# A spectral GFNet branch beside a gated ReGLU branch on one core: half-row passes grouped by three units, one ring of six PSUM banks, and 24 small copies issued by ScalarE

## The chip, the cores and the metric

The kernel runs on one core of one Trainium2 chip. The metric is the device time of one execution in microseconds (us). Three runs of the kernel before took 446.72, 446.89 and 446.91 us, a median of 446.89 us.

## What is computed

The reference adds three things: the input, a spectral filter of its layer norm, and a gated feed-forward block of its layer norm.

```python
def _A_ref(x, w_r, w_i):
    X = jnp.fft.rfft2(x, axes=(-2, -1)) * (w_r + 1j * w_i)
    return jnp.fft.irfft2(X, s=(S, D), axes=(-2, -1))

def _B_ref(x, W_gate, W_up, W_down):
    gate = jnp.einsum("bsd,df->bsf", x, W_gate)
    up = jnp.einsum("bsd,df->bsf", x, W_up)
    h = gate * (gate > 0) * up
    return jnp.einsum("bsf,fd->bsd", h, W_down)

xn = _layernorm(x, axis=-1)
return x + _A_ref(xn, A_w_r, A_w_i) + _B_ref(xn, B_W_gate, B_W_up, B_W_down)
```

S = 2048 rows, D = 448 columns, F = 1792 hidden columns, all in float32.

## The kernel before

**Arithmetic.** Every float32 operand of a matmul is split into a float16 high part and a float16 low part, and a product is three matmuls: high by high, high by low, low by high. A matmul streams up to 512 columns into one PSUM bank, which holds 512 float32 values in each of 128 partitions; there are 8 banks.

**The gated branch.** The rows are cut into four chunks of 512 (order 0, 2, 1, 3), the hidden columns into 14 tiles of 128, taken in groups of 5, 5 and 4. A *unit* is one hidden tile on one chunk: 56 units. A unit has two outputs, the gate (g = 0) and the up projection (g = 1), one bank each. D = 448 is three and a half contraction tiles, so an output takes 10 matmuls with all 128 rows (`SEQ`, line 706, issued by `gu_full`, line 712) and one with 64 rows, the *half pass* (`gu_half`, line 718). The half pass of the gate uses rows 0 to 63 of the array and that of the up projection rows 64 to 127 (`TOP`, line 707).

Units are taken in pairs (`mates`, line 969). The first of a pair, the *opener*, runs its 20 full matmuls; then four half passes stand together, two of its mate and two of its own (`gu_halves`, line 740); then the mate runs its 20 (`gu_unit`, line 730). I call the half passes that stand together a *stand*. There are 28 stands of four.

After a unit, `gu_post` (line 766) works on its outputs: ScalarE reads the gate bank and writes relu(gate) (line 752, "relu" below), VectorE reads the up bank and multiplies (line 756, "times"), ScalarE makes the high part (line 760) and VectorE the low part (line 764). When all units of a group and chunk are done, four down projections (`dn_mm`, line 775, lines 783 and 790) of 15 or 12 matmuls each use them.

**PSUM.** Units take a tile of two banks from a pool of two (`gu`), down projections one bank from a pool of two (`dn`, line 778), everything of the spectral branch one bank from a pool of two (`fx`, line 145): 4 + 2 + 2 banks.

**The spectral branch** is a list of background items (`bg`, from line 801): layer norm of chunks 1 and 3, transposes by DMA into the tiles `T`, discrete Fourier transforms as matmuls (lines 357 and 389), then butterflies on VectorE in four stages over 18 buffers (`bfly`, line 391), multiplication by the filter, the inverse butterflies, and the inverse transforms (lines 611 and 632). The butterfly with factor 1 (p = 0, lines 393 to 398) writes the sum into a free buffer and the difference over `b`, the second operand, and puts `a` at the end of the list of free buffers, from which the next one is popped. Two kinds of small copies inside the chip's memory are issued by SyncE: 16 row copies (`row_in`, line 559; the row that all blocks share) and, per pair of spectra, two exchange copies that mirror rows (`swap`, lines 544 and 545 before the filter, 547 and 548 behind it; line 548 is already ScalarE's).

**The order** is made at build time. Each matmul, VectorE and ScalarE step is issued by the program in the order of the units; background items are dealt out between them by a credit in us of VectorE time (`room`, line 1100, and the search for the share `load` in lines 1105 to 1110, which asks that the rooms of all units add up to the need of the background list), and a scheduler with its own cost model then sets the final order of each engine's queue. The opening (line 30) is an order written out by hand; it ends with the first units of chunk 0 and the stand named `hp4`. At run time each engine works through its own queue in that order and waits on semaphores.

Of the kernel before, what the change touches and what calls it, by code (L numbers as in the profile page):

```python
# [21 lines left out]
XW = 4 * GW  # L22
# [111 lines left out]
def tile_gfnet_reglu(ctx: ExitStack, tc: tile.TileContext, x, xr, wgu, wd, wf, wrow, ident, c_fd, c_fm, c_im, c_row, c_id,  # L134
# [10 lines left out]
    def fx():  # L145
        return psum.tile([128, 512], F32, name="fx", bufs=2)
# [184 lines left out]
    def ln_tp(n2, tiles):  # L331
        if n2 not in tp:
            tp[n2] = fx().bitcast(F16).rearrange("p (a b) -> p a b", b=128)
        for a in tiles:
            P.transpose(tp[n2][:, a, :], tt[n2][:, a, :], id_t)
# [9 lines left out]

    zps, eo, X, Xh, yps, cur = {}, {}, {}, {}, {}, {}

    def f_dft(n2):
        q, j = n2 % 4, n2 // 4
        js = slice(128 * j, 128 * (j + 1))  # L350
        ps = fx()
# [33 lines left out]
    def f_sdft(n2):  # L385
        y = yps[n2] = fx()[:, 0:XW].rearrange("p (g c k) -> p g c k", g=4, c=2)
# [4 lines left out]
    def bfly(a, b, p, sgn):  # L391

        if p == 0:
            t = free.pop()
            V.tensor_tensor(t, a, b, op=OP.add)  # L395
            V.tensor_tensor(b, a, b, op=OP.subtract)  # L396
            free.append(a)
            return t, b
        t = free.pop()
        if p == 4:  # L400
# [5 lines left out]
            free.append(b)  # L406
# [132 lines left out]
    def swap(key, k):  # L539
# [3 lines left out]
        if key == "X":  # L543
            nc.sync.dma_start(t[1:64], u[65:128])
            nc.sync.dma_start(t[64:128], u[0:64])
# [10 lines left out]
    def row_in(j):  # L556
        for par in range(2):
            p = 16 * j + 8 * par
            nc.sync.dma_start(row[p:p + 8, 0, :], cur["s1", j, par][64:65].rearrange("p g c k -> p (g c) k"))
# [7 lines left out]
    def row_dft(d):  # L567
        y = state["rowps"] = fx()
# [35 lines left out]
    def i_sdft(n2):  # L604
        ps = fx()
# [20 lines left out]
    def i_ddft(n2):  # L626
        ps = fx()
# [81 lines left out]
    def gu_open(f, q):  # L709
        hps[f, q] = psum.tile([128, 2, 512], F32, name="gu", bufs=2)  # L710

    def gu_full(f, q, gs, cs, start, stop, seq=SEQ):
        for g in gs:
            for i, (a, b) in enumerate(seq):
                last["P"] = P.matmul(hps[f, q][:, g, cs], wt[f, g][:, a, :], Tq[q][:, b, cs],  # L715
                                     start=(start and i == 0), stop=(stop and i == len(seq) - 1)).ins

    def gu_half(f, q, g, start, prev):
# [3 lines left out]
        m = P.matmul(hps[f, q][:, g, 0:512], wt[f, g][rows, 7, :], Tq[q][rows, b, :], start=start, stop=not start).ins  # L722
# [7 lines left out]
    def gu_unit(f, q, mate):  # L730
# [7 lines left out]
        gu_halves(f, q, mate)  # L738

    def gu_halves(f, q, mate):  # L740
        gu_open(*mate)
        m = last["P"]
        for i in range(4):
            with tc.high_priority(offset=2000 if i else 0):
                m = gu_half(*((f, q) if i > 1 else mate), 1 - i % 2, i < 2, m)
        opened.add(mate)
# [3 lines left out]
    def gu_relu(f, q):  # L750
        g1s[f, q] = mt([128, 512], F32, "g1", 3)
        last["A"] = A.activation(g1s[f, q], hps[f, q][:, 0, :], AF.Relu, scale=2.0 ** -22).ins  # L752

    def gu_times(f, q):
        g1 = g1s[f, q]
        last["V"] = V.scalar_tensor_tensor(g1, hps[f, q][:, 1, :], 2.0 ** -22, g1, op0=OP.mult, op1=OP.mult).ins  # L756
# [18 lines left out]
    def dn_mm(fs, n2, c0=0, c1=D):  # L775
        q, j = n2 % 4, n2 // 4
        js = slice(128 * j, 128 * (j + 1))
        ps = psum.tile([128, 512], F32, name="dn", bufs=2)
# [180 lines left out]
    gseq = [("gu", g, f, q) for g, fs in enumerate(groups) for q in CHUNKS for f in fs]  # L959
    units, pend = [], []  # L960
# [239 lines left out]
```

## Time and profile before

| | us |
|---|---|
| median of three runs | 446.89 |
| the profiled execution, its own time | 446.92 |
| its span, first to last instruction | 445.1 |
| TensorE busy | 438.4 (98%) |
| VectorE busy | 373.5 (84%) |
| ScalarE busy | 178.9 (40%) |
| GpSimd busy | 32.9 (7%) |

The 1.8 us between the span and the profiled time lie around the program. "Busy" of TensorE counts a matmul from its start to its modelled end, and successive matmuls overlap, so its pace is read from starts: how far the start of one group is from the start of the next. A weight load (PEld) is an instruction of its own that overlaps the matmul before it. Line numbers with an L are those of the kernel; a queue's own work (issuing a DMA) carries a q behind the engine.

### The profile page before, as it was taken

The page shows a single profiled execution, that of the slowest core. Times are in us where ns is not written, and L with a number is a line of the kernel's source. Part 1 is how long each engine was busy: PE and PEld are TensorE (multiplying, and loading weights), DVE is VectorE, ACT ScalarE, POOL GpSimd, SP SyncE. Part 2 cuts the span into 40 slices and gives each one's busy share as a digit, 9 for nine tenths or more (in the row PEclk, how much of TensorE's full clock was granted, in tenths as well). Part 3 has the DMA queues.
Part 4 walks back from the last instruction along what each step waited for, and adds up shares of the span by engine and source line. Part 5 has one row for each costly group of instructions (what it writes and reads, how often), then busy time and mean ns, then how long its engine had stood idle before and what let it go on. Part 6 is the DMA issues. An engine that isn't in the chain of part 4 may idle for free.

```text
span 445.1 us, 7091 instructions
## 1 busy us (share of the span) xinstructions
PE 438.4 (98%) x2630; PEld 218.8 (49%) x2630; DVE 373.5 (84%) x802; ACT 178.9 (40%) x365; POOL 32.9 (7%) x97
## 2 busy tenths in 40 slices
PE   8999999999999999999999999999999999999997
PEld 3543554444546444444444444444444455556565
DVE  5988696998858979999999999896997997766364
ACT  5886252351543666043233145344142242233230
POOL 2431031040000120000000010000000000000000
DMA  8929966041001261432220021000001333231113
GB/s 271 323 52 282 371 217 119 1 90 41 0 14 61 95 222 34 133 105 62 85 80 6 1 84 55 0 13 0 14 0 42 93 96 90 55 96 34 63 43 124
DMA packets 37115, 39.72 MB, mean 89 GB/s; under 512 B 17927, under 2 KB 32473, under 8 KB 37081
## 3 DMA queue, kind: packets, MB, share of 16 engines
q1 hardware_dynamic: 35928, 37.40, 27.4%
q10 hardware_dynamic: 1152, 1.87, 2.1%
q8 instruction: 20, 0.33, 0.3%
q14 instruction: 15, 0.11, 0.1%
HBM read 24.45 MB, written 3.67 MB: 63 GB/s over the span
## 4 chain that ended last, share of the span: by engine, by line
PE 91%; DVE 3%; DMA 2%; ACT 1%; issue 1%; POOL 1%; SPq 0%; ACTq 0%
PE gu L715 50%; PE dn L783 29%; PE gu L722 3%; PE fx L611 2%; PE fx L357 2%; PE fx L632 2%; PE fx L389 2%; DMA y<-in_xr 1%; DMA T<-tt 1%; DVE bst L248 1%; DVE wt L669 1%; DVE y L291 0%; DVE g L756 0%; ACT T L341 0%; DVE tt L320 0%
## 5 line engine op out<-in xcount | busy, mean ns | idle before, releaser
L715 PE MATMUL gu<-T,wt 128*128 128x512 f16 (+1 forms) x1140 | 256.1, 375 | 0.0
L715 PEld LDWEIGHTS <-wt 128*128 128x128 f16 x1140 | 108.7, 98 | 129.8 <-issue 9.3
L783 PE MATMUL dn<-wdt,h 128*128 128x448 f16 (+2 forms) x684 | 136.4, 349 | 0.0
L783 PEld LDWEIGHTS <-h 128*128 128x128 f16 x684 | 65.8, 98 | 59.9
L752 ACT ACTIVATE g<-gu 128x512 f32<-128x512 f32 x56 | 33.2, 594 | 115.1 <-PE gu L722 77.4
L760 ACT ACTIVATE h<-g 128x512 f16<-128x512 f32 x56 | 35.0, 627 | 47.3 <-DVE g L756 47.3
L756 DVE SCALAR_TENSOR_TENSOR g<-gu,g 128x512 f32<-128x512 f32 x56 | 38.5, 687 | 11.4 <-ACT g L752 11.3
L790 DVE SCALAR_TENSOR_TENSOR xy<-dn,dsc,xy 128x448 f32<-128x448 f32 (+2 forms) x49 | 32.9, 671 | 15.1 <-PE dn L783 14.8
L764 DVE TENSOR_TENSOR h<-g,h 128x512 f16<-128x512 f32 x56 | 38.5, 689 | 4.9 <-ACT h L760 4.8
L665 ACT ACTIVATE wt<-wst,wsc 128x512 f16<-128x512 f32 x28 | 19.1, 716 | 15.7 <-DVE wsc L196 15.7
L669 DVE SCALAR_TENSOR_TENSOR wt<-wst,wsc,wt 128x512 f16<-128x512 f32 x28 | 20.5, 749 | 0.0
L637 DVE SCALAR_TENSOR_TENSOR xy<-fx,fsc,xy 128x448 f32<-128x448 f32 x16 | 10.8, 681 | 10.7 <-PE fx L632 10.7
L189 POOL PARTITION_ALL_REDUCE wm<-wm x15 | 7.8, 521 | 158.9 <-ACT junk L186 158.9
L396 DVE TENSOR_TENSOR y<-y 128x456 f32<-128x456 f32 x22 | 13.9, 631 | 4.8 <-DMA row<-y 4.5
L722 PE MATMUL gu<-T,wt 64*128 64x512 f16 x112 | 17.0, 381 | 0.8 <-DMA T<-tt 0.7
L186 ACT ACTIVATE junk<-wst 128x512 bf16<-128x512 f32 x28 | 17.4, 622 | 0.2
L595 ACT ACTIVATE vt<-y,fsc 128x912 f16<-128x912 f32 x8 | 8.4, 1052 | 20.7 <-PE fx L611 12.3
L618 ACT ACTIVATE wf<-fx 114x512 f16<-114x512 f32 x16 | 9.4, 588 | 17.4 <-PE fx L611 16.6
L553 DVE TENSOR_TENSOR y<-y,sw 128x456 f32<-128x456 f32 x16 | 10.1, 628 | 5.7 <-DMA sw<-y 5.7
L395 DVE TENSOR_TENSOR y<-y 128x456 f32<-128x456 f32 x22 | 13.8, 628 | 0.2
L611 PEld LDWEIGHTS <-vt 128*128 128x128 f16 x192 | 12.0, 98 | 3.3
L611 PE MATMUL fx<-wf,vt 128*128 128x128 f16 x192 | 13.2, 219 | 0.0
(115 smaller groups left out, 431.4 us busy)
## 6 DMA issues: line engine op xcount, KB each, us to landing
wst<-in_wgu SPq DMA_DIRECT2D x28, 256.0 KB
wf<-in_wf SPq DMA_DIRECT2D x8, 456.0 KB
sw<-y SPq DMA_DIRECT2D x16, 224.4 KB
y<-in_xr SPq DMA_DIRECT2D x16, 224.0 KB
xy<-in_x SPq DMA_DIRECT2D x16, 224.0 KB
out<-xy SPq DMA_DIRECT2D x15, 224.0 KB
wdst<-in_wd SPq DMA_DIRECT2D x14, 224.0 KB
sw<-y SPq DMA_DIRECT2D x8, 228.0 KB
```

Of the source, the lines that this page charges most:

```text
L186: A.activation(o, src, AF.Square, scale=SQ, accum_out=acc)
L611: P.matmul(o, v[:, h, w], m[:, c, :], start=(i == 0), stop=(i == 2), skip_group_check=True)
L665: A.activation(w[:, 0:4, :], wst[f, g], AF.Copy, scale=wsc[f, g])
L669: V.scalar_tensor_tensor(w[:, 4:8, :], st, sc, w[:, 0:4, :], op0=OP.mult, op1=OP.subtract)
L715: last["P"] = P.matmul(hps[f, q][:, g, cs], wt[f, g][:, a, :], Tq[q][:, b, cs], start=(start and i == 0), stop=(stop and i == len(seq) - 1 ...
L722: m = P.matmul(hps[f, q][:, g, 0:512], wt[f, g][rows, 7, :], Tq[q][rows, b, :], start=start, stop=not start).ins
L752: last["A"] = A.activation(g1s[f, q], hps[f, q][:, 0, :], AF.Relu, scale=2.0 ** -22).ins
L756: last["V"] = V.scalar_tensor_tensor(g1, hps[f, q][:, 1, :], 2.0 ** -22, g1, op0=OP.mult, op1=OP.mult).ins
L760: A.activation(ht[f, q][:, 0, :], g1s[f, q], AF.Copy)
L764: V.tensor_tensor(h[:, 1, :], g1s.pop((f, q)), h[:, 0, :], op=OP.subtract)
L783: last["P"] = P.matmul(ps[:, 0:c1 - c0], ht[f, q][:, a, js], wdt[f][:, b, c0:c1], start=(i == 0), stop=(i == n - 1)).ins
L790: last["V"] = V.scalar_tensor_tensor(o, dps[n2][:, 0:c1 - c0], dsc[:, g:g + 1], o, op0=OP.mult, op1=OP.add).ins
```

## The change

Five edits.

1. `mates` now lists units in groups: two groups of two, sixteen of three, two of two (20 groups for 56 units). The opener's stand holds the half passes of both mates and its own: six in a stand of a group of three. Every later full matmul of a unit is ordered behind the last half pass issued. The down projections of a finished chunk are issued behind a mate instead of behind every second unit.
2. `gu` and `dn` share one ring of six banks (`RINGS`, `bank`); a unit takes two tiles of one bank.
3. The butterfly with factor 1 writes the difference over `a`, and the freed buffers go to the front of the list, so that they are reused last.
4. The 16 row copies and one of the two exchange copies before the filter (8) are issued by ScalarE.
5. The search for the share asks for 3.0 us more than the need.

```diff
--- before.py
+++ after.py
@@ -144,4 +144,7 @@

-    def fx():
-        return psum.tile([128, 512], F32, name="fx", bufs=2)
+    RINGS = {'gu': ('gu', 6), 'dn': ('gu', 6), 'fx': ('fx', 2)}
+
+    def bank(name="fx"):
+        tag, n = RINGS[name]
+        return psum.tile([128, 512], F32, name=name, tag=tag, bufs=n)

@@ -332,3 +335,3 @@
         if n2 not in tp:
-            tp[n2] = fx().bitcast(F16).rearrange("p (a b) -> p a b", b=128)
+            tp[n2] = bank().bitcast(F16).rearrange("p (a b) -> p a b", b=128)
         for a in tiles:
@@ -344,3 +347,2 @@

-
     zps, eo, X, Xh, yps, cur = {}, {}, {}, {}, {}, {}
@@ -350,3 +352,3 @@
         js = slice(128 * j, 128 * (j + 1))
-        ps = fx()
+        ps = bank()
         T = Tq[q]
@@ -385,3 +387,3 @@
     def f_sdft(n2):
-        y = yps[n2] = fx()[:, 0:XW].rearrange("p (g c k) -> p g c k", g=4, c=2)
+        y = yps[n2] = bank()[:, 0:XW].rearrange("p (g c k) -> p g c k", g=4, c=2)
         m, xh = fm_t[n2 % 8][:, n2 // 8], Xh[n2 % 8][:, n2 // 8]
@@ -395,5 +397,5 @@
             V.tensor_tensor(t, a, b, op=OP.add)
-            V.tensor_tensor(b, a, b, op=OP.subtract)
-            free.append(a)
-            return t, b
+            V.tensor_tensor(a, a, b, op=OP.subtract)
+            free.insert(0, b)
+            return t, a
         t = free.pop()
@@ -405,3 +407,3 @@
             V.tensor_tensor(a[:, :, 1], a[:, :, 1], b[:, :, 0], op=o1)
-            free.append(b)
+            free.insert(0, b)
             return t, a
@@ -544,3 +546,3 @@
             nc.sync.dma_start(t[1:64], u[65:128])
-            nc.sync.dma_start(t[64:128], u[0:64])
+            nc.scalar.dma_start(t[64:128], u[0:64])
         else:
@@ -558,3 +560,3 @@
             p = 16 * j + 8 * par
-            nc.sync.dma_start(row[p:p + 8, 0, :], cur["s1", j, par][64:65].rearrange("p g c k -> p (g c) k"))
+            nc.scalar.dma_start(row[p:p + 8, 0, :], cur["s1", j, par][64:65].rearrange("p g c k -> p (g c) k"))

@@ -567,3 +569,3 @@
     def row_dft(d):
-        y = state["rowps"] = fx()
+        y = state["rowps"] = bank()
         for d in ((0, 1), (2,))[d]:
@@ -604,3 +606,3 @@
     def i_sdft(n2):
-        ps = fx()
+        ps = bank()
         v, m = vt[n2 % 8][:, n2 // 8], im_t[n2 % 8][:, n2 // 8]
@@ -626,3 +628,3 @@
     def i_ddft(n2):
-        ps = fx()
+        ps = bank()
         h = pgh[n2]
@@ -709,3 +711,3 @@
     def gu_open(f, q):
-        hps[f, q] = psum.tile([128, 2, 512], F32, name="gu", bufs=2)
+        hps[f, q] = [bank("gu") for g in range(2)]

@@ -714,4 +716,6 @@
             for i, (a, b) in enumerate(seq):
-                last["P"] = P.matmul(hps[f, q][:, g, cs], wt[f, g][:, a, :], Tq[q][:, b, cs],
+                m = last["P"] = P.matmul(hps[f, q][g][:, cs], wt[f, g][:, a, :], Tq[q][:, b, cs],
                                      start=(start and i == 0), stop=(stop and i == len(seq) - 1)).ins
+                if "opened" in state and "half" in last:
+                    tc.add_manual_dep(m, last["half"].name, NOSYNC, reason="half passes stand together")

@@ -721,3 +725,3 @@
         rows, b = TOP[g]
-        m = P.matmul(hps[f, q][:, g, 0:512], wt[f, g][rows, 7, :], Tq[q][rows, b, :], start=start, stop=not start).ins
+        m = P.matmul(hps[f, q][g], wt[f, g][rows, 7, :], Tq[q][rows, b, :], start=start, stop=not start).ins
         if "opened" in state:
@@ -729,3 +733,3 @@

-    def gu_unit(f, q, mate):
+    def gu_unit(f, q, mates):

@@ -737,11 +741,15 @@
         gu_full(f, q, gs, cs, True, False)
-        gu_halves(f, q, mate)
+        gu_halves(f, q, mates)

-    def gu_halves(f, q, mate):
-        gu_open(*mate)
+    def gu_halves(f, q, mates):
         m = last["P"]
-        for i in range(4):
+        vs = [v[2:] for v in mates] + [(f, q)]
+        for i in range(2 * len(vs)):
+            v = vs[i // 2]
+            if i % 2 == 0 and v != (f, q):
+                gu_open(*v)
+                opened.add(v)
             with tc.high_priority(offset=2000 if i else 0):
-                m = gu_half(*((f, q) if i > 1 else mate), 1 - i % 2, i < 2, m)
-        opened.add(mate)
+                m = gu_half(*v, 1 - i % 2, v != (f, q), m)
+        last["half"] = m

@@ -751,3 +759,3 @@
         g1s[f, q] = mt([128, 512], F32, "g1", 3)
-        last["A"] = A.activation(g1s[f, q], hps[f, q][:, 0, :], AF.Relu, scale=2.0 ** -22).ins
+        last["A"] = A.activation(g1s[f, q], hps[f, q][0], AF.Relu, scale=2.0 ** -22).ins

@@ -755,3 +763,3 @@
         g1 = g1s[f, q]
-        last["V"] = V.scalar_tensor_tensor(g1, hps[f, q][:, 1, :], 2.0 ** -22, g1, op0=OP.mult, op1=OP.mult).ins
+        last["V"] = V.scalar_tensor_tensor(g1, hps[f, q][1], 2.0 ** -22, g1, op0=OP.mult, op1=OP.mult).ins

@@ -777,3 +785,3 @@
         js = slice(128 * j, 128 * (j + 1))
-        ps = psum.tile([128, 512], F32, name="dn", bufs=2)
+        ps = bank("dn")
         n = 3 * len(fs)
@@ -959,6 +967,11 @@
     gseq = [("gu", g, f, q) for g, fs in enumerate(groups) for q in CHUNKS for f in fs]
+    mates, inner, k = {}, set(), 0
+    for n in [2, 2] + [3] * 16 + [2, 2]:
+        mates[gseq[k]] = gseq[k + 1:k + n]
+        inner.update(gseq[k + 1:k + n])
+        k += n
     units, pend = [], []
-    for k, u in enumerate(gseq):
+    for u in gseq:
         units.append(u)
-        if k % 2 and pend:
+        if u in inner and pend:
             units += pend
@@ -968,3 +981,2 @@
     units += pend
-    mates = {u: v for u, v in zip(gseq[::2], gseq[1::2])}
     first = {}
@@ -1050,5 +1062,6 @@
     def gu_slab(f, g):
-        if f % 2 == 0 and g == 0:
+        first = ("gu", 0, f, q) in mates
+        if first and g == 0:
             gu_open(f, q)
-        gu_full(f, q, (g,), slice(0, 512), f % 2 == 0, f % 2 == 1)
+        gu_full(f, q, (g,), slice(0, 512), first, not first)

@@ -1064,4 +1077,4 @@
             piece(f"{tag}{f}", fn, f, q)
-        if f % 2 == 0:
-            piece(f"hp{f}", gu_halves, f, q, mates["gu", 0, f, q][2:])
+        if ("gu", 0, f, q) in mates:
+            piece(f"hp{f}", gu_halves, f, q, mates["gu", 0, f, q])
         for g in range(2):
@@ -1083,3 +1096,3 @@
         G.memset(warm, 0.0)
-        wps = psum.tile([128, 512], F32, name="dn", bufs=2)
+        wps = bank("dn")
         gu_open(0, q)
@@ -1108,3 +1121,3 @@
         need = sum(c - m * p for c, p, _, _ in bg)
-        lo, hi = (m, hi) if sum(room(i, m) for i in range(RAMP, last_gu)) < need else (lo, m)
+        lo, hi = (m, hi) if sum(room(i, m) for i in range(RAMP, last_gu)) < need + 3.0 else (lo, m)
     load[0] = hi
@@ -1124,3 +1137,3 @@
             run_bg(until=marks["T", q])
-            gu_unit(f, q, (mates.get(u) or (0, 0, None, None))[2:])
+            gu_unit(f, q, mates.get(u))
         else:
```

The program that results has as many instructions of each kind on each compute engine as before; the order differs. Lines are shifted: 722 becomes 726, 715 becomes 717, 783 becomes 791, 752 becomes 760, 632 becomes 634, 357 becomes 359.

**A stand of half passes, on TensorE.** `gu` are the banks of units (the number names the unit's tile), `wt` their weights, `T` the input chunk. Before, in the middle of the kernel's last third:

```order
L715 MATMUL gu_3639<-T2_63,wt_3174 128x512
L722 LDWEIGHTS wt_3222
L722 MATMUL gu_3660<-T2_63,wt_3222 128x512
L722 LDWEIGHTS wt_3219
L722 MATMUL gu_3660<-T2_63,wt_3219 128x512
L722 LDWEIGHTS wt_3174
L722 MATMUL gu_3639<-T2_63,wt_3174 128x512
L722 LDWEIGHTS wt_3171
L722 MATMUL gu_3639<-T2_63,wt_3171 128x512
L715 LDWEIGHTS wt_3219
```

Now, a stand of a group of three:

```order
L726 LDWEIGHTS wt_2023
L726 MATMUL gu_2264<-T0_62,wt_2023 128x512
L726 LDWEIGHTS wt_2018
L726 MATMUL gu_2263<-T0_62,wt_2018 128x512
L726 LDWEIGHTS wt_2088
L726 MATMUL gu_2268<-T0_62,wt_2088 128x512
L726 LDWEIGHTS wt_2083
L726 MATMUL gu_2267<-T0_62,wt_2083 128x512
L726 LDWEIGHTS wt_1966
L726 MATMUL gu_2242<-T0_62,wt_1966 128x512
L726 LDWEIGHTS wt_1961
L726 MATMUL gu_2241<-T0_62,wt_1961 128x512
```

Each unit has its two half passes side by side; there are now six without a full matmul between them.

**The same stand in two of the sixteen groups of three.** This one opens the unit of chunk 3 that stands among units of chunk 1 (`gu_1425` and `gu_1424`); the other, in the last third, has six matmuls of line 613 in the same place (`fx_3731`).

```order
L726 MATMUL gu_1421<-T1_64,wt_546 128x512
L726 LDWEIGHTS wt_520
L726 MATMUL gu_1420<-T1_64,wt_520 128x512
L726 LDWEIGHTS wt_243
L726 MATMUL gu_1425<-T3_65,wt_243 128x512
L359 LDWEIGHTS T1_64
L359 MATMUL fx_1436<-fd_t_83,T1_64 128x114
L726 LDWEIGHTS wt_221
L726 MATMUL gu_1424<-T3_65,wt_221 128x512
L726 LDWEIGHTS wt_422
L726 MATMUL gu_1399<-T1_64,wt_422 128x512
L726 LDWEIGHTS wt_456
```

A matmul with all 128 rows has come between the two half passes of one unit. In the program before, all 28 stands are whole.

**The first exchange copies, on ScalarE.** `sw` are the exchange buffers, lines 760 and 768 the relu and the high part of a unit. Before, this stretch of ScalarE's queue had no copy: it went from the filter's sign flip (then line 496) to a high part and a relu. Now:

```order
L189 ACTIVATE junk_2292,small_72<-wf2_2043 128x456
L498 ACTIVATE wf2_2043<-wf2_2043 128x2x114
L547 DMA sw0_2044<-y_66 64x2x456
L547 DMA sw1_2045<-y_66 64x2x456
L547 DMA sw2_2046<-y_66 64x2x456
L760 ACTIVATE g1_2235<-gu_2012 128x512
L768 ACTIVATE h_2238<-g1_2235 128x512
```

Three copies, each of which waits for its butterfly on VectorE, now stand ahead of a relu. A copy stands directly ahead of a relu in five places in all: this one with three, and four with one each.

**The end of TensorE's queue.** Before, the last matmuls are the 160-column part of the last down projection, with the 288-column part ahead of it; now the 288-column part is last.

## Rows read from the trace of the kernel before

**Rows 1.** The page: busy us (share of the span) of each engine.

```profile
PE 438.4 (98%) x2630; PEld 218.8 (49%) x2630; DVE 373.5 (84%) x802; ACT 178.9 (40%) x365; POOL 32.9 (7%) x97
```

**Rows 2.** The chain that ended last: shares; then in order of time: start, us, what.

```profile
PE 91%; DVE 3%; DMA 2%; ACT 1%; issue 1%; POOL 1%; SPq 0%; ACTq 0%
...
35.27 3.25 DMA T<-tt
...
38.65 0.61 PE gu L722 x4
39.26 4.42 PE gu L715 x20
```

**Rows 3.** Busy by window, 39 to 443 us (engines, granted clock, DMA share, GB/s).

```profile
39.00:443.00 404.00, 403.25 (x2441) 201.98 (x2437) 341.12 (x704) 148.46 (x299) 20.12 (x49) 1.00 0.26 77
```

**Rows 4.** Timeline of TensorE, 282 to 300 us: start, us to the modelled end, what.

```profile
285.14 0.59 PE L715 MATMUL gu<-T,wt 128*128 128x512 f16 x2
285.67 0.60 PE L722 MATMUL gu<-T,wt 64*128 64x512 f16 x4
286.21 4.49 PE L715 MATMUL gu<-T,wt 128*128 128x512 f16 x20
290.53 1.30 PE L783 MATMUL dn<-wdt,h 128*128 128x448 f16 x6
```

**Rows 5.** Timeline of the weight loads in the same stand.

```profile
285.67 0.11 PEld L722 LDWEIGHTS <-wt 64*128 64x128 f16 x4 [0.42 <-issue]
286.20 0.76 PEld L715 LDWEIGHTS <-wt 128*128 128x128 f16 x5 [0.42 <-issue]
```

**Rows 6.** Groups by line: xcount | busy us, mean ns | idle before, releaser.

```profile
L722 PE MATMUL gu<-T,wt 64*128 64x512 f16 x112 | 17.0, 381 | 0.8 <-DMA T<-tt 0.7 <-DVE wt L669 0.2
L722 PEld LDWEIGHTS <-wt 64*128 64x128 f16 x112 | 3.2, 94 | 12.1 <-issue 11.3 <-DVE wt L669 0.4 <-DVE y L291 0.4
L752 ACT ACTIVATE g<-gu 128x512 f32<-128x512 f32 x56 | 33.2, 594 | 115.1 <-PE gu L722 77.4 <-PE gu L715 37.5 <-DVE h L764 0.2
L756 DVE SCALAR_TENSOR_TENSOR g<-gu,g 128x512 f32<-128x512 f32 x56 | 38.5, 687 | 11.4 <-ACT g L752 11.3
L396 DVE TENSOR_TENSOR y<-y 128x456 f32<-128x456 f32 x22 | 13.9, 631 | 4.8 <-DMA row<-y 4.5
```

**Rows 7.** Timeline of the end, VectorE: start, us, what, idle before.

```profile
441.40 0.52 DVE L790 SCALAR_TENSOR_TENSOR xy<-dn,dsc,xy 128x288 f32<-128x288 f32 x1 [0.20 <-PE dn L783]
442.29 0.38 DVE L790 SCALAR_TENSOR_TENSOR xy<-dn,dsc,xy 128x160 f32<-128x160 f32 x1 [0.37 <-PE dn L783]
```

**Rows 8.** DMA rate, 440 to 446 us in 40 slices, and the last stores' sizes.

```profile
GB/s 0 48 323 394 382 311 72 0 0 0 0 0 0 84 346 382 382 299 121 369 407 123 0 90 333 124 0 0 0 0 0 0 0 0 0 0 0 0 0 0
...
out<-xy SPq DMA_DIRECT2D x1, 144.0 KB
out<-xy SPq DMA_DIRECT2D x1, 80.0 KB
```

**Rows 9.** Issues by line: duration ns min/median/max, first and last start us.

```profile
L548 ACTq DMA_DIRECT2D sw<-y x8: 597/600/667, 341.6 to 390.4; - x8
L559 SPq DMA_DIRECT2D row<-y x16: 619/657/804, 67.0 to 160.5; - x16
L545 SPq DMA_DIRECT2D sw<-y x8: 645/648/708, 175.7 to 268.4; - x8
```

**Rows 10.** Waits: who waited for whom: us in total, times, longest us.

```profile
ACT h L760 <- DVE g L756: 47.3, 39, 3.6
DVE y L396 <- DMA row<-y: 4.5, 4, 1.8
```

## The prediction

> **What bounds the kernel now.** I read the page first: TensorE is busy 98% of the span, VectorE 84%, ScalarE 40% [rows 1]. A busy TensorE need not be the limit, so the chain of waits came next: 91% of it is TensorE, and its last piece on another engine before the tail is the landing of the transposes of chunk 2 at 38.5 us [rows 2]. From there to the end the window has TensorE busy 403.25 of 404.00 us, at a granted clock of 1.00 [rows 3]. Then I took the pace from starts in the timeline: 20 full matmuls from 286.21 to 290.53, or 0.216 us each [rows 4]. TensorE keeps this pace up to the tail; the one thing in the rows that costs it anything is the stand of half passes. So a change is worth what it takes from TensorE's own stream, less the waits that it puts in. VectorE and ScalarE count only where TensorE would wait for them.
>
> **What a stand costs.** In rows 4 the second full matmul starts at 285.14 + 0.216 = 285.36, the first half pass at 285.67, the next full matmul at 286.21. From full to full that is 0.85 us. The full matmul itself takes 0.216 of it, and four half passes, two by two side by side, 2 x 0.216 = 0.43. The rest, 0.20 us, is lost at the two ends, about 0.1 at each. The weight loads show the same: before the first half pass and before the full matmul behind the stand the load engine sat idle for 0.42 us [rows 5], and 26 such gaps before half passes make 11.3 us [rows 6], where within a run of full matmuls each load lies under the matmul ahead.
>
> **The change part by part.**
>
> *Groups of three.* 28 stands become 20, and the 56 pairs of half passes stay. I take 0.216 us for a third pair too. Saved: 8 x 0.20 = 1.60 us. All stands but the first two (and the end of `hp4`) lie in the full stretch, so all of it is on the path; `hp4`'s third pair is 0.22 us that its group gets back at its end.
>
> *Two broken stands.* In the queue as built, two of the sixteen stands of three have full-row matmuls between the two half passes of one unit. That stand runs a pair, a lone half pass, the way out, the foreign matmul, the way in, a pair of half passes of two different units, and a lone one: four steps of 0.216 and 2 x 0.20 in place of three steps and 0.20. That is 0.42 us each, 0.83 us for both. The lower bound is 0.20 each, should each lone half pass run beside something; I take the upper value, since queues run in order and the matmul between uses all rows.
>
> *The end.* The last matmuls are now 288 columns wide. Their eviction takes 0.52 us in place of 0.38 [rows 7], +0.14, and the last store has 144 KB in place of 80; 64 KB at the 382 GB/s that the stores reach here [rows 8] is 0.17 us. Together +0.31, at least 0.14 if the store's length is hidden.
>
> *Ring of six.* TensorE gains nothing, as it waited for no bank. What it can lose: behind the last unit of a group the next opener takes 20 x 0.216 = 4.32 us, and about 0.3 us later the stand's last pair needs that unit's banks, so its gate bank, complete 2.16 us before the unit's end, has 2.16 + 4.6 = 6.8 us until times must be over. Relu takes 0.594 us and times 0.687 [rows 6]; the longest that ScalarE ever waited for times is 3.6 us [rows 10], so the latest case was 0.6 + 3.6 = 4.2 us. Cost 0, with 2.6 us to spare.
>
> *Copies on ScalarE.* 24 issues of 0.60 us, the duration of ScalarE's own exchange copies [rows 9], are 14.4 us of its queue; on SyncE they took about 0.65 us each [rows 9]. ScalarE has room for that (148 us of 404 busy [rows 3]). What is queued behind a copy is relu, in five places. One copy adds 0.6 us to the 4.2, three add 2.0 with their waits to check: 4.8 and 6.2 against 6.8. Cost 0, but at the place with three only 0.6 us of cover is left, and a copy that waits for its butterfly eats it. The transposes on SyncE, which had row copies between them, start up to 0.7 us sooner each; TensorE waited for transposes once, in the opening, where no copy is in the way. Gain 0.
>
> *Butterflies.* VectorE's 22 subtractions waited 4.5 us for row copies that still read what they overwrite [rows 10], nearly all of the idle time before line 396 [rows 6]. The older operand's copy is over sooner. The saving is at most 4.5 us of VectorE's idle time and at worst the same lost; either way off the path. Cost 0.
>
> *Pace.* 3.0 us of background work spread over the middle come earlier. VectorE's total is unchanged, TensorE is the limit to the end: 0. It lengthens VectorE's backlog by part of 3.0 us at worst, which counts against the 2.6 us above.
>
> Sum: -1.60 + 0.83 + 0.31 = -0.46 us. Against the profiled execution of 446.92 us that is 446.46; its median stands 0.03 us lower, so I say **446.4 us**. The forecast's own range: with the low bounds of the broken stands and the end 446.92 - 1.60 + 0.40 + 0.14 = 445.9, and with some tenths of small waits 446.9.
>
> **The rivals.**
>
> *F, the clean gain.* The broken stands and the end cost nothing, and 446.92 - 1.60 = 445.3 us. For it: the stands' ends are the only loss in TensorE's stream. Against: the foreign matmuls stand in the queue between half passes, and the trace shows a loss at every change between the two kinds. Chance 0.12.
>
> *H, the third pair's weights.* All four loads of a stand lie in 0.11 us at its start [rows 5], two for each half of the array. A third load per half has no example in this trace. If it waits until the second pair is over, each of 16 stands loses one load of 94 ns [rows 6]: +1.5 us, 447.9. Against: full matmuls hide their loads at the same pace. Chance 0.07.
>
> *S, relu behind copies: slower.* ScalarE's queue runs in order. A copy waits for its butterfly, relu behind it is late, times is late, and the third unit's bank is not free when the stand comes. It decides from the point where the copies' own wait passes 0.6 us (three copies) or 2.0 us (one). With the 3.6 us of backlog of rows 10 as that wait, the first exchange loses 3.0 us and the other four places 1.6 each, 9.4 at most; I take the first alone, 446.4 + 3.0 = 449.4 us. For it: banks of the third unit are a need that pairs did not have, and relu's queue never held a copy in that stretch. Against: the butterfly stands ahead of times in VectorE's own queue, so a late one would have delayed times anyway. The Trainium skill, in "TensorEngine Tiling (Array Packing)", section "Gotcha 1: PSUM Pressure", says that row tiling raises the pressure on PSUM, since row tiles write to different banks and software must keep them in step. By that rule six half passes, which hold all six banks at once, would be where TensorE waits; the trace, with four banks and no wait, neither shows nor excludes it. Chance 0.16.
>
> **How the numbers follow.** A measurement here tells 0.2%, or 0.9 us, from no change: faster is under 446.0, slower over 447.8. The forecast has 0.65, of which 0.07 lies under 446.0. F adds 0.12 to faster: 0.2. H lies on the upper border and is halved; S is slower: 0.2 with its half. The rest is 0.6. The range goes from F, 445.3, to just above H, 448.0; it leaves out S and the outer tails, 2 in 10.
>
> **What would show it.** In the profile after: 18 whole stands, each with 0.20 us of loss and 0.22 us per pair, and two broken ones 0.42 us longer. Between 39 us and the tail TensorE's starts should have no other gap. Under H the third pair starts 0.3 us behind the second; under S ScalarE shows relu ending behind a copy and TensorE idle at a half pass, first at the first exchange (some 180 us). Idle TensorE anywhere else in the middle, over 1 us in all, would prove the forecast wrong, as would broken stands that cost nothing.

## The result, and the profile after

The changed kernel took 447.76 us (median of 22 runs, 447.02 to 448.44), the kernel before beside it 446.85 us (22 runs, 446.48 to 447.20): a ratio of 1.0018, 95% interval 1.0012 to 1.0025. The forecast was 446.4 us. The changed kernel is slower by 0.9 us where a gain of 0.5 was forecast: the time lies in the range given (to 448.0), its direction was missed. The profiled execution took 447.88 us, its span is 446.1.

From the page of the changed kernel, busy time and the shares of the chain, to be held against [rows 1, 2]; then the window from 39 to 443 us with the columns of [rows 3]:

```profile
PE 437.5 (98%) x2630; PEld 220.1 (49%) x2630; DVE 372.2 (83%) x802; ACT 178.0 (40%) x365; POOL 34.9 (8%) x97
...
PE 81%; DVE 10%; DMA 4%; issue 1%; ACT 1%; SPq 1%; POOL 1%; DVEq 0%; ACTq 0%
```

```profile
39.00:443.00 404.00, 402.78 (x2439) 203.37 (x2435) 339.22 (x704) 147.51 (x299) 21.73 (x49) 1.00 0.26 77
```

The busy times have hardly moved and the granted clock is 1.00 again. What moved is the chain: TensorE falls from 91% to 81%, VectorE rises from 3% to 10%. TensorE now waits for VectorE somewhere in the middle.

**The stands** are as forecast. Timeline of TensorE, changed kernel: a whole stand of six, then a broken one.

```profile
67.57 0.38 PE L717 MATMUL gu<-T,wt 128*128 128x512 f16 x1
67.88 0.82 PE L726 MATMUL gu<-T,wt 64*128 64x512 f16 x6
68.64 2.33 PE L717 MATMUL gu<-T,wt 128*128 128x512 f16 x10
...
112.17 0.60 PE L726 MATMUL gu<-T,wt 64*128 64x512 f16 x3
112.71 0.22 PE L359 MATMUL fx<-fd_t,T 128*128 128x114 f16 x1
112.86 0.60 PE L726 MATMUL gu<-T,wt 64*128 64x512 f16 x3
113.40 1.34 PE L359 MATMUL fx<-fd_t,T 128*128 128x114 f16 x23
```

Six half passes take 68.64 - 67.88 = 0.76 us where four took 0.54 [rows 4]: the third pair costs 0.22. The loss at the two ends is the old one, 67.88 - 67.57 - 0.216 = 0.09 and 0.76 - 3 x 0.216 = 0.11. The broken stand, cut by one short foreign matmul, takes 113.40 - 112.17 = 1.23 us, 0.47 more than the whole one: the 0.42 of the forecast and the 0.05 that the foreign matmul takes itself.

**Two new stalls** of TensorE. The first, at a stand near 201 us (timeline of TensorE, some lines left out; the bracket is the idle time and what ended it):

```profile
166.77 11.51 PE L791 MATMUL dn<-wdt,h 128*128 128x448 f16 x60
...
186.21 0.82 PE L726 MATMUL gu<-T,wt 64*128 64x512 f16 x6
186.96 13.12 PE L717 MATMUL gu<-T,wt 128*128 128x512 f16 x60
200.01 0.60 PE L726 MATMUL gu<-T,wt 64*128 64x512 f16 x3
201.16 0.59 PE L726 MATMUL gu<-T,wt 64*128 64x512 f16 x3 [0.54 <-DVE g L764]
201.68 4.92 PE L717 MATMUL gu<-T,wt 128*128 128x512 f16 x22
```

The stand at 186 us takes 0.75 us, the one at 200 us 1.67: three half passes ran, the fourth waited for times (line 764) of an earlier unit, and the pair it belongs to no longer ran side by side. 0.92 us are lost. Times ran late because VectorE's queue was late; VectorE's timeline, changed kernel:

```profile
165.68 0.63 DVE L397 TENSOR_TENSOR y<-y 128x456 f32<-128x456 f32 x1 [1.62 <-DMA row<-y]
...
179.80 0.63 DVE L555 TENSOR_TENSOR y<-y,sw 128x456 f32<-128x456 f32 x1 [1.15 <-DMA sw<-y]
...
199.22 0.68 DVE L703 SCALAR_TENSOR_TENSOR wdt<-wdst,wds,wdt 128x448 f16<-128x448 f32 x1
199.82 0.69 DVE L772 TENSOR_TENSOR h<-g,h 128x512 f16<-128x512 f32 x1
200.42 0.69 DVE L764 SCALAR_TENSOR_TENSOR g<-gu,g 128x512 f32<-128x512 f32 x1
```

From 179.80 us to the stall VectorE works without a pause. Ahead of that it stood idle twice, 1.62 us for a row copy and 1.15 us for the first exchange copy. In the kernel before, the idle times at these two places are 0.31 and 0.56 us:

```profile
162.54 0.64 DVE L396 TENSOR_TENSOR y<-y 128x456 f32<-128x456 f32 x1 [0.31 <-DMA row<-y]
...
179.50 0.63 DVE L553 TENSOR_TENSOR y<-y,sw 128x456 f32<-128x456 f32 x1 [0.56 <-DMA sw<-y]
```

ScalarE passes VectorE's lateness on. The relu of the late unit (line 760) stands behind a high part (line 768) that waits for the times before it; ScalarE of the changed kernel:

```profile
197.13 0.63 ACT L768 ACTIVATE h<-g 128x512 f16<-128x512 f32 x1 [1.29 <-DVE g L764]
197.67 0.58 ACT L760 ACTIVATE g<-gu 128x512 f32<-128x512 f32 x1
```

The second stall, at 361 us: TensorE, VectorE and ScalarE of the changed kernel, one fence each.

```profile
359.16 1.03 PE L717 MATMUL gu<-T,wt 128*128 128x512 f16 x4
360.79 0.83 PE L613 MATMUL fx<-wf,vt 128*128 128x128 f16 x12 [0.59 <-DVE wf L624]
```

```profile
356.12 0.69 DVE L764 SCALAR_TENSOR_TENSOR g<-gu,g 128x512 f32<-128x512 f32 x1 [1.36 <-ACT g L760]
358.95 0.63 DVE L555 TENSOR_TENSOR y<-y,sw 128x456 f32<-128x456 f32 x1 [2.15 <-DMA sw<-y]
359.50 0.63 DVE L556 TENSOR_TENSOR y<-y,sw 128x456 f32<-128x456 f32 x1
360.05 0.69 DVE L624 SCALAR_TENSOR_TENSOR wf<-fx,wf 114x512 f16<-114x512 f32 x1
```

```profile
353.57 1.81 ACTq L550 DMA_DIRECT2D sw<-y  x2
355.49 0.60 ACT L760 ACTIVATE g<-gu 128x512 f32<-128x512 f32 x1 [3.53 <-DVE y L407]
```

The inverse transform needs its bank (fx), which the low part wf (line 624) has to read first; wf stands in VectorE's queue behind a butterfly that waits 2.15 us for its exchange copy. TensorE starts 1.63 us after the matmul group ahead, which has four steps of 0.216: 0.76 us lost. Relu stands behind two copies on ScalarE here, but these two were ScalarE's in the kernel before as well.

The waits as a list (in total, times, longest), against [rows 10], and the end on VectorE, against [rows 7]:

```profile
ACT h L768 <- DVE g L764: 71.8, 39, 6.1
...
DVE y L555 <- DMA sw<-y: 7.0, 4, 2.1
```

```profile
442.32 0.38 DVE L798 SCALAR_TENSOR_TENSOR xy<-dn,dsc,xy 128x160 f32<-128x160 f32 x1
442.95 0.52 DVE L798 SCALAR_TENSOR_TENSOR xy<-dn,dsc,xy 128x288 f32<-128x288 f32 x1 [0.25 <-PE dn L791]
```

ScalarE's longest wait for times went from 3.6 to 6.1 us. The tail behind TensorE's last matmul is 3.17 us, 0.29 longer than before (forecast 0.31). The account: -1.60 for the stands, +0.83 for the broken ones, +0.92 and +0.76 for the stalls, +0.29 for the end, -0.09 since the first whole stretch starts that much sooner, makes +1.1; the span grew by 0.95.

### The profile page after: what moved, and what is told of

It reads as the page before. It is cut to its first block, busy times and chain, and to the rows that moved or that the text cites. A ratio compares the mean times of both kernels' runs of the same rounds, so it can differ in the third digit from the quotient of the medians.

```text
span 446.1 us, 7122 instructions
## 1 busy us (share of the span) xinstructions
PE 437.5 (98%) x2630; PEld 220.1 (49%) x2630; DVE 372.2 (83%) x802; ACT 178.0 (40%) x365; POOL 34.9 (8%) x97
## 4 chain that ended last, share of the span: by engine, by line
PE 81%; DVE 10%; DMA 4%; issue 1%; ACT 1%; SPq 1%; POOL 1%; DVEq 0%; ACTq 0%
PE gu L717 44%; PE dn L791 26%; PE gu L726 3%; PE fx L613 2%; PE fx L359 2%; PE fx L634 2%; PE fx L391 2%; DVE g L764 1%; DMA row<-y 1%; DMA y<-in_xr 1%; DMA sw<-y 1%; DMA T<-tt 1%; DVE h L772 1%; DVE wt L671 1%; DVE bst L251 1%
## 5 line engine op out<-in xcount | busy, mean ns | idle before, releaser
L717 PE MATMUL gu<-T,wt 128*128 128x512 f16 (+1 forms) x1140 | 252.4, 375 | 0.0
L791 PE MATMUL dn<-wdt,h 128*128 128x448 f16 (+2 forms) x684 | 132.1, 349 | 0.0
```

Of the source, the lines that this page charges most:

```text
L717: m = last["P"] = P.matmul(hps[f, q][g][:, cs], wt[f, g][:, a, :], Tq[q][:, b, cs], start=(start and i == 0), stop=(stop and i == len(seq) ...
L791: last["P"] = P.matmul(ps[:, 0:c1 - c0], ht[f, q][:, a, js], wdt[f][:, b, c0:c1], start=(i == 0), stop=(i == n - 1)).ins
```

## The experiments

The theories, once the two traces had been compared. **W**: VectorE's idle waits for row and exchange copies make times and wf late, and the stalls follow. **Rivals**: the copies' place on ScalarE; the pace; the butterflies; the groups and the ring by themselves (the third unit's bank, or the blocks of 60 down projections that the shared ring makes, as at 166.77 above; in the kernel before, the same stretch has pieces of 18, 15 and fewer between units).

Twelve kernels, each beside the kernel before, whose median was 446.77 to 446.94. First what they showed, from one profiled execution each: VectorE's idle waits for copies between 160 and 186 us, what TensorE lost at a single gap of over 0.25 us between 180 and 205 us, and the time from the last matmul's end to the end of the span. The last two columns are over all runs of a kernel.

| kernel | copy waits | gaps of TensorE | tail | median us | ratio |
|---|---|---|---|---|---|
| before | 0.87 | 0 | 2.88 | 446.85 | 1 |
| changed | 2.77 | 0.70 | 3.17 | 447.76 | 1.0018 |
| e1 groups and ring alone | 4.91 | 0.42 | 4.78 | 449.99 | 1.0074 |
| e2 copies on SyncE | 2.92 | 1.11 | 3.17 | 447.88 | 1.0025 |
| e3 no pace | 3.11 | 1.11 | 4.78 | 451.18 | 1.0088 |
| e4 old butterflies | 4.56 | 1.98 | 3.17 | 449.24 | 1.0053 |
| e5 whole stands | 2.10 | 0 | 3.16 | 447.37 | 1.0008 |
| e6 pairs, one ring | 3.79 | 0.67 | 4.80 | 449.20 | 1.0048 |
| e7 the other three edits | 1.97 | 1.04 | 2.88 | 448.07 | 1.0027 |
| e8 down projections two and two | 4.15 | 1.19, 0.51 | 3.17 | 448.87 | 1.0046 |
| e9 no copies | 0 | 0 | 3.16 | 446.37 | 0.9988 |
| e10 inverse butterfly later | 2.64 | 0.56 | 4.79 | 449.43 | 1.0055 |
| e11 wf ahead | 2.81 | 0.72 | 3.16 | 445.92 | 0.9976 |
| e12 e11, row copies split, end | 2.92 | 1.11 | 4.23 | 447.80 | 1.0016 |

The first two columns do not rise and fall together: e1 waits longest for copies, 4.91 us, and loses 0.42 in this window, while e7 waits 1.97 and loses 1.04. So the table alone shows no cause; e9 below has to. The stall at 361 us lies outside the window; of the kernels that keep the copies, only the changed one, e2, e5 and e10 have it.

**Parts alone, and parts undone.** e1 is the kernel before with the first two edits, e7 the kernel before with the other three; e2, e3 and e4 each take one edit back from the changed kernel.

```diff
@@ e2 @@
-            nc.scalar.dma_start(t[64:128], u[0:64])
+            nc.sync.dma_start(t[64:128], u[0:64])
...
-            nc.scalar.dma_start(row[p:p + 8, 0, :], ...
+            nc.sync.dma_start(row[p:p + 8, 0, :], ...
@@ e3 @@
-        lo, hi = (m, hi) if ... < need + 3.0 else (lo, m)
+        lo, hi = (m, hi) if ... < need + 0.0 else (lo, m)
@@ e4 @@
-            V.tensor_tensor(a, a, b, op=OP.subtract)
-            free.insert(0, b)
-            return t, a
+            V.tensor_tensor(b, a, b, op=OP.subtract)
+            free.append(a)
+            return t, b
...
```

> The kernel before with the groups of three and the ring of six alone (no copies on ScalarE, old butterflies, no pace). Its queue has two broken stands too (one by a discrete Fourier matmul of line 359, one by the row transform of line 573). All theories: stands -1.6, broken stands +0.8, end +0.3 against the kernel before. Theory V (VectorE's backlog, fed by the pace and by late copies, makes times and wf late; the ring only passes it on): no stall of TensorE over 0.3 us, -0.5 us, ratio to before 0.999. Rival G (the third unit's bank is needed too early whatever the other edits): a stall of 0.5 us or more at a stand, some 1.0 to 1.5 us of stalls in all, ratio 1.001 to 1.002.

> The kernel before with the butterflies, the copies on ScalarE and the pace of the change, in pairs and with its own rings. The forecast's terms for these three are 0: 446.8, 1.000 of before. Rival (late copies stall TensorE wherever the bank is waited for): a stall over 0.3 us at a stand or at an inverse transform, 447.5 or more, 1.0015. Should the pace shorten the tail also here, under 446.5.

e1: 449.99 us, interval of the ratio 1.0062 to 1.0086, past both theories. It has a stall at 187 us, one of 0.65 us at 402 us, one of 0.45 us at 442 us, and a tail longer by 1.6 us than the changed kernel's. e7: 448.07 us (1.0016 to 1.0038), the time that the rival gave (447.5 or more), but its one stall is at neither of the rival's places: it is at a full matmul of a unit.

```profile
190.76 0.38 PE L715 MATMUL gu<-T,wt 128*128 128x512 f16 x1
192.02 1.24 PE L715 MATMUL gu<-T,wt 128*128 128x512 f16 x5 [0.88 <-DVE g L756]
```

So neither half of the change is free: +3.2 us alone, +1.2 us alone, +0.9 us together. The effects do not add up.

> The changed kernel with the 16 row copies and the 8 exchange copies back on SyncE. Theory C (copies on ScalarE hold relu up and land late): both stalls go (the one at 201 us at the third unit's half pass, 0.70 us, and the one at 361 us at the inverse transform, 0.76 us), 1.4 us faster than the changed kernel, 0.999 of before. Theory V: the stall at 361 us may go, since relu stood behind copies there (-0.7), the one at 201 us stays, since relu was in time there: 447.0. If the copies play no part: as the changed kernel, 1.002 of before.

> The changed kernel with the pace at the need itself (3.0 us less). Theory P (the pace makes VectorE's backlog): the stall at 201 us goes, 0.7 us faster than the changed kernel, 447.0 or 1.000 of before. If the pace plays no part: 1.002 of before, both stalls there.

> The changed kernel with the butterflies of before (the difference over the newer operand, freed buffers reused first). Its queue has one broken stand in place of two: -0.4 us by the forecast's price. If the butterflies save VectorE waits for the row copies (up to 4.5 us in the kernel before), VectorE's backlog is larger without them and the stall at 201 us grows or stays: 447.4 or more. Rival B (the changed order of the buffers causes the long waits for exchange copies): the stall at 361 us goes as well, 446.6.

e2: 447.88 us (1.0016 to 1.0033), no different from the changed kernel. The stall near 200 us stays, at 1.11 us, and of the one at 361 us 0.37 us are left. Who issues the copies makes no difference to the time, but it moves the waits: VectorE's wait for the row copy falls from 1.62 to 0.59 us, and those for exchange copies grow from 1.15 to 2.33. e3: 451.18 us (1.0075 to 1.0102), the opposite of both expectations: the pace is worth 3.4 us here. In the profiled execution, which is the fastest of five (449.75 us), the stall near 201 us is 1.11 us and the one at 361 us is gone; the granted clock is 1.00 from 39 to 443 us. What is lost shows at the end; VectorE there:

```profile
442.62 1.28 DVE L639 SCALAR_TENSOR_TENSOR xy<-fx,fsc,xy 128x448 f32<-128x448 f32 x2 [0.24 <-PE fx L634]
443.81 1.39 DVE L798 SCALAR_TENSOR_TENSOR xy<-dn,dsc,xy 128x448 f32<-128x448 f32 x3
```

The last inverse transforms come behind the last down projection, and four evictions (the second of line 639, three of line 798) run behind the last matmul's end at 443.17 us, where the changed kernel has one. That is 1.6 us of tail and 0.3 us at the last matmul's end; the rest of the 3.4 us is in executions that were not profiled, and stays open. e4: 449.24 us (1.0037 to 1.0069): by the medians the new butterflies are worth 1.5 us. Without them VectorE waits 4.56 us for copies and TensorE 1.98 us at the next stand; the stall at 361 us is gone, as Rival B had it, but not its gain. The six runs lie in two groups, three from 448.11 to 448.80 us at a mean granted clock of 1.0 and three from 449.67 to 450.60 at 0.996. The profiled one is of the first group, whose median is 0.7 us above the changed kernel; where the others lose the rest is open.

**Stands and down projections.** In e5 every matmul of the spectral branch gets the new dependency (here the one line that adds it); e8 has it too.

```diff
@@ e5 @@
+            tc.add_manual_dep(m.ins, last["half"].name, NOSYNC, reason="half passes stand together")
@@ e6 @@
-    for n in [2, 2] + [3] * 16 + [2, 2]:
+    for n in [2] * 28:
@@ e8 @@
-            units += pend
-            pend = []
+            units += pend[:2]
+            pend = pend[2:]
...
```

> The changed kernel with every matmul of the spectral branch that is issued behind a stand ordered behind the stand's last half pass: all 20 stands are whole, the rest of the queue as it was. If a broken stand costs 0.42 us each, as the forecast has it: 0.83 us faster than the changed kernel, 446.9 or 1.000 of before. Rival: the foreign matmuls filled a wait for the third unit's bank, so the time comes back as a stall at these two stands: 447.6, 1.0015 of before.

> The changed kernel with all 56 units in pairs again (28 stands of four, none broken), still on one ring of six banks. By the stands alone 8 x 0.2 - 0.83 = +0.8 us against the changed kernel. Theory D (the shared ring puts the down projections of a chunk into one block of 60 matmuls, so units follow each other without a pause and VectorE falls behind): the stalls remain, though a pair holds fewer banks; 448.3 or more, 1.003 to 1.004 of before. Rival U (only the third unit's bank is needed too early): the stall near 200 us goes, 447.5, 1.0015 of before.

> The changed kernel with whole stands where the order allows it (one broken stand is left) and the four down projections of a chunk issued two and two behind different units, so that blocks of 60 matmuls become blocks of 30. Theory D: the stall near 200 us goes, 0.4 us for one broken stand less and 0.7 us for the stall: 446.6, under 1.000 of before. Rival U (the third unit's bank, whatever the order of the down projections): 447.3 with a stall of 0.5 us or more at a stand.

e5: 447.37 us (0.9999 to 1.0017), between the two, and by the intervals not clear of the changed kernel. The stands are whole and the stall at 200 us is gone from its profile, but the one at 360 us has grown from 0.76 to 1.43 us, with VectorE's wait for the exchange copy (2.34 us):

```profile
358.00 1.03 PE L723 MATMUL gu<-T,wt 128*128 128x512 f16 x4
360.30 0.83 PE L140 MATMUL fx<-wf,vt 128*128 128x128 f16 x12 [1.27 <-DVE wf L630]
```

e6: 449.20 us (1.0034 to 1.0061). With pairs no stand waits near 200 us, but the same lateness shows at the next place that needs a result, a down projection that waits for h:

```profile
201.76 1.11 PE L791 MATMUL dn<-wdt,h 128*128 128x448 f16 x5
203.38 1.95 PE L791 MATMUL dn<-wdt,h 128*128 128x448 f16 x9 [0.50 <-ACT h L768]
```

So the third unit's bank is where the lateness shows, not what makes it (U falls). By the account, 1.60 - 0.83 for the stands, -0.92 - 0.76 + 0.67 for the stalls, +1.63 for the tail and -0.13 for an earlier start of the first whole stretch make +1.3 against the changed kernel; measured +1.4. e8: 448.87 us (1.0033 to 1.0058). Blocks of 30 are no cure (D falls as the one cause), and they show what else the shared ring does: a stand now waits for the eviction of a down projection.

```profile
186.82 0.38 PE L732 MATMUL gu<-T,wt 64*128 64x512 f16 x1
188.22 0.59 PE L732 MATMUL gu<-T,wt 64*128 64x512 f16 x3 [1.03 <-DVE xy L804]
```

**The copies themselves.** e9 is the changed kernel without any row or exchange copy (and without the copies of the row back into the exchange buffers): it leaves these parts of the spectral branch out.

```diff
@@ e9 @@
-            nc.sync.dma_start(t[1:64], u[65:128])
-            nc.scalar.dma_start(t[64:128], u[0:64])
...
-            nc.scalar.dma_start(row[p:p + 8, 0, :], ...
...
-            G.memset(t[0:1], 0.0)
+            G.memset(t, 0.0)
```

> The changed kernel without the row copies and the exchange copies (their targets are set once instead; the spectral part is then not computed rightly): same queue, same two broken stands, but VectorE never waits for a copy. Theory W (VectorE's idle waits for the landing of row and exchange copies, 1.62 and 1.15 us ahead of 201 us and 2.15 us at 359 us, are what makes times and the high part late): both stalls of TensorE go, 1.4 us faster than the changed kernel, 446.3 or 0.999 of before. Rival K (VectorE has simply too much work between 180 and 201 us, copies or not): the stall at 201 us stays at 0.5 us or more, 447.0 or above.

446.37 us, ratio 0.9988 (0.9979 to 0.9997): W holds, K falls. The same two stands are broken and no stall is left; TensorE's timeline at the place of either stall, and ScalarE's wait for times:

```profile
200.21 0.82 PE L723 MATMUL gu<-T,wt 64*128 64x512 f16 x6
200.96 2.33 PE L714 MATMUL gu<-T,wt 128*128 128x512 f16 x10
...
357.78 1.50 PE L610 MATMUL fx<-wf,vt 128*128 128x128 f16 x24
```

```profile
ACT h L765 <- DVE g L761: 57.2, 37, 4.0
```

ScalarE's longest wait for times falls from 6.1 to 4.0 us. How much VectorE gets done from 165 to 180 us, third pair of numbers after the comma (columns as in [rows 3]), in the changed kernel and in e9:

```profile
165.00:180.00 15.00, 15.00 (x78) 7.54 (x77) 13.14 (x30) 8.31 (x25) 1.68 (x1) 1.00 0.21 51
```

```profile
165.00:180.00 15.00, 15.00 (x78) 7.53 (x77) 14.96 (x34) 8.21 (x25) 1.27 (x1) 1.00 0.02 8
```

13.14 us against 14.96: the 1.8 us that VectorE stood idle are the backlog that it carries into the stand. Without copies VectorE's instructions are no shorter (times takes 685 ns against 687), so it is the waits that count and not a slower VectorE. And 446.37 us agrees with the 446.4 forecast for a kernel in which no bank is late; its interval is 0.4 us to either side.

**Towards a better kernel.** All three start from e5. e10 moves `i_pair` and `i_hi` from the even half step to just ahead of `i_lo`. e11 orders each inverse butterfly behind the wf issued last. e12 adds to e11 that of two row copies one is SyncE's and one ScalarE's, and that the 160-column part of the last down projection is ordered last.

```diff
@@ e11 @@
-        pair("U", m, -1)
+            with tc.issue_after(state["wfi"]):
+                pair("U", m, -1)
@@ e12 @@
-            nc.scalar.dma_start(row[p:p + 8, 0, :], ...
+            (nc.sync, nc.scalar)[par].dma_start(row[p:p + 8, 0, :], ...
```

> The changed kernel with whole stands (as in the run with 20 whole stands) and each butterfly of the inverse exchange issued half a step later, just ahead of the low part that needs it, so that the copies have some 2.3 us more to land. Theory W: the stall at 360 us (1.43 us with whole stands) goes, nothing else changes: 447.4 - 1.4 = 446.0, 0.998 of before, under both kernels. Rival: the wait only moves to the next user of that butterfly (the inverse transform's matmuls), 447.0 or more.

> The changed kernel with whole stands and one more edit: in VectorE's queue each butterfly of the inverse exchange is ordered behind the low part (wf) issued last before it, so that wf no longer stands behind a butterfly that waits for its copies. Theory W' (TensorE's stall at 360 us is wf held up in VectorE's queue by a butterfly that waits for its copies): the stall of 1.43 us goes, the tail stays 3.2 us, 447.4 - 1.4 = 446.0, 0.998 of before. Rival: the butterfly is itself needed next, the wait only moves behind it: 447.0 or more, with a stall of TensorE near 362 us.

> The same with two edits more: of each two row copies one is issued by SyncE and one by ScalarE, and the 160-column part of the last down projection is ordered behind the 288-column part as in the kernel before. Theory W: VectorE's wait for the row copies near 165 us (0.96 us with whole stands) shrinks, no stall at 200 us; the end gives back 0.31 us: 445.7, 0.997 of before. Rival: no stall was left to take away, only the end counts: 0.3 us under the run without these two.

e10: 449.43 us (1.0042 to 1.0069), a miss. The order of wf and the waiting butterfly did not change, so 1.18 us of stall stay at 360 us, and the end became that of e3. e11: 445.92 us, ratio 0.9976 (0.9962 to 0.9989): the stall at 360 us is gone and the time is that of W', below both kernels. The same instruction that waited 2.15 us for its copy now finds it landed, two wf later; TensorE and VectorE of e11:

```profile
356.78 1.03 PE L727 MATMUL gu<-T,wt 128*128 128x512 f16 x4
357.65 1.50 PE L140 MATMUL fx<-wf,vt 128*128 128x128 f16 x24
```

```profile
356.26 0.68 DVE L634 SCALAR_TENSOR_TENSOR wf<-fx,wf 114x512 f16<-114x512 f32 x1
...
360.70 0.68 DVE L634 SCALAR_TENSOR_TENSOR wf<-fx,wf 114x512 f16<-114x512 f32 x1
361.30 0.62 DVE L561 TENSOR_TENSOR y<-y,sw 128x456 f32<-128x456 f32 x1
```

Its profiled execution (446.27 us) has the stall at 200 us again, 0.72 us, which e5's had not and W' did not expect, and a first whole stretch that starts 0.38 us sooner; that the time came out within 0.1 us is in part luck. Its fastest run took 445.07. e12: 447.80 us (1.0007 to 1.0025), a miss twice over. With row copies on both queues VectorE waits less for them (0.62 us) and more for the exchange copy (2.31), and holding back the narrow part sent an inverse transform to the very end: tail 4.23 us.

## Why the prediction was wrong

- *What bounds the kernel*: right, and it held only as long as VectorE kept up. TensorE's pace was the bound in the kernel before; in the changed one 1.7 us come from VectorE.
- *Groups of three*: right. The loss per stand is 0.20 us still, the third pair 0.22. H is refuted.
- *Two broken stands*: right in the trace. e5, which takes them away, gained 0.39 us by the medians, which is not clear of noise; the other stall grew.
- *The end*: right, +0.29 against +0.31.
- *Ring of six, cost 0 with 2.6 us to spare*: **this is the step that failed.** The budget was right. The unit whose bank was late ended 40 matmuls into the run at 186.96, at 195.6 us, and its gate bank 10 matmuls sooner, at 193.4. Times was over at 201.11, 7.7 us later, 0.9 us past the budget of 6.8; that is the stall. What failed was the other side, the 4.2 us of the latest case. It was taken from rows 10 of the kernel before, as if VectorE's lateness were a constant, and it let relu begin as soon as the gate bank was complete; here relu began 4.2 us after that, at 197.67, behind a high part that waited for VectorE. VectorE's lateness is a backlog, made by idle waits for copies ahead of a stretch in which it has no pause. e9 shows it: without copies the stalls go. Why the waits are longer than before is shown in part only: with the copies on SyncE the one for the row copy is 0.59 us in place of 1.62 (e2), but the others grow.
- *Copies on ScalarE, 0*: right in the time (e2), not in the waits, which moved. The cover of 0.6 us was counted at the wrong place: what delayed times was not relu behind a copy but VectorE, waiting for a copy to land.
- *Butterflies, 0*: wrong by 1.5 us by the medians, 0.7 us by the faster group of runs (e4). VectorE's 4.5 us of waits for row copies were put off the path because TensorE did not wait in the trace of before. They were one source of the backlog. With the new butterflies 1.6 us of them are left, in e4 all 4.5.
- *Pace, 0*: wrong by 3.4 us, and with the other sign than feared (e3). In this order it keeps the inverse transforms ahead of the last down projection; e6 and e10 have the pace and yet the long tail. That TensorE is the limit to the end says nothing of which evictions come behind its last matmul.
- *The rivals*: S was right in kind, a bank not free when the stand comes, and wrong in place, mechanism and price. At 180 us, where it was expected, TensorE did not wait; near 201 us it did, for 0.92 us and not 3.0, with relu long over (its run ended at 198.25 us). At 361 us relu did wait 3.53 us behind copies, but behind two that were ScalarE's before, and TensorE waited for wf. F is refuted by the broken stands.

The Trainium skill, in "TensorEngine Tiling (Array Packing)", section "Gotcha 1: PSUM Pressure", has it that row tiles need several banks kept in step. The trace agrees as to where TensorE waits, at a half pass, 0.54 us at 201.16. e6, with fewer banks held, waits at the next place, and e9, with all six, does not wait.

What stays open: why the copy waits are 0.87 us in one order and 2 to 5 us in the others, beyond that each order puts other VectorE work beside the copies; the other half of the pace's 3.4 us, and the two groups of e4's runs. A kernel in which the row copies read from a buffer of their own was not tried.

## What to carry to other kernels

A slack that is read from one order of work need not hold in another: before a buffer is called free in time, look for what the engine that frees it waits for upstream, and add those waits to its backlog. Here VectorE, which ran without a pause from 179.80 us, handed its idle time on to TensorE 20 us later. In an in-order queue, order an instruction that waits for a transfer behind the ones that are ready (e11: 1.4 us by the medians, for one line on top of e5).

## What was not expected of the hardware

A very small copy inside the chip's memory lands hardly sooner than one over a hundred times its size. In the chain of waits of the changed kernel (start, us, what) a row copy, which moves 1.8 KB from one partition, takes as long as an exchange copy, which moves over 220 KB from some 64:

```profile
160.52 5.07 DMA row<-y
...
175.12 4.57 DMA sw<-y
```

In the chain of e2, where SyncE issues both, they take 3.81 and 4.81 us.

And a stand that stops between the two half passes of a unit loses more than its wait: 0.92 us at 200 us for 0.70 us of gap, since the pair then no longer runs side by side.
